# Modulation products with 32 equal moving columns and two more dummy matmuls ahead of the first attention unit

## Chip, cores, metric

One core of a Trainium2 chip. The metric is the device time of one execution in microseconds (us). Each execution also has a *span*, from the first to the last instruction that the profile records, and a granted TensorE clock (1.000 is full).

## The reference

One block of a conditioned transformer: a modulation vector of six slices from `c`, a layer norm scaled and shifted by it, attention with cached keys and values, and an MLP.

```python
mod = (_silu(c) @ w_mod).reshape(c.shape[0], 6, 1, -1)      # c: (1, 512), w_mod: (512, 3072)
sa, ca, ga, sb, cb, gb = (mod[:, 0].copy(), ..., mod[:, 5].copy())
h = _layernorm(x, axis=-1) * (1 + ca) + sa                  # x: (1, 2048, 512)
x = x + ga * _A_ref(h, A_k_cache, A_v_cache, A_wq, A_wo)    # 32 heads, 512 keys
h = _layernorm(x, axis=-1) * (1 + cb) + sb
x = x + gb * _B_ref(h, B_w1, B_w2)                          # 512 -> 1792 -> 512, ReLU
```

## The kernel before

TensorE works without a break once the first scores are computed. Everything that matters here is the way to that point: the two modulation slices `sa` and `ca` (32 products of one column each), the transposes of the first four normalised tiles, scaling and shifting (`mod_half`, on VectorE and ScalarE, whose results are the pieces hT that the Q projections read), the first Q projections in halves, the first scores. `warm(n)` issues dummy products of 512 columns that only keep TensorE busy.

```python
def warm(n, gate=(), bk=7):
    for i in range(n):
        mm(bank[bk], ones[:, :], ones[:, 0:1].to_broadcast([P, QB]), True, True, [R_ones] + list(gate), [bk], i == n - 1)

def mod_cols_mm(which, bk):                     # 4 x 2 x 4 = 32 products, all into one bank
    ...
                fs.append(lambda sl=sl, c2=c2, cc=cc, col=sl * DC + c2, last=last: mm(
                    bank[bk][:, col:col + 1], wm[sl][:, cc, c2 * P:(c2 + 1) * P], sc_bf[:, cc:cc + 1],
                    cc == 0 and sl == 0 and c2 == 0, last, [R_sc, wm_res(sl, cc)], [bk], last))

def mod_cols_evac(which, bk):                   # modc <- the eight columns + (0 or 1)
    ...
# --- the order of the start (cut to what the argument touches) ---
warm(10)                                        # first warm-up
silu_exp(5)
ln_stat(0); warm(3, [R_mv[0]]); ln_stat(1); warm(2, [R_mv[1]])
...
for f in mod_cols_mm(0, QBK): f()
ln_tposes(0, TB[0])
mod_cols_evac(0, QBK)
ln_tposes(1, TB[0])
warm(2, bk=1)                                   # the two dummies among the transposes
ln_norm(2)
mod_half(0, 0, DVE); mod_half(0, 2, ACT)
ln_tposes(2, TB[1]); ln_tposes(3, TB[1])
mod_half(0, 1, DVE); mod_half(0, 3, ACT)
q_half(0, 0, CC_ORDER, QBK)                     # four products, one for each hT piece
mod_half(1, 0, DVE); mod_half(1, 2, ACT); mod_half(1, 1, DVE); mod_half(1, 3, DVE)
q_evac_half(0, 0, QBK, ACT)                     # qT <- psQ on ScalarE
q_half(1, 0, CC_ORDER, 5); q_evac_half(1, 0, 5, ACT)
s_half(0, 0); s_half(1, 0)                      # the first score products
...
```

Of the kernel before, what the change touches and what calls it, by code (L numbers as in the profile page):

```python
# [9 lines left out]
ALU = mybir.AluOpType  # L10
# [127 lines left out]
def build_general(nc, es, A_x, A_k_cache, A_v_cache, A_wq, A_wo, B_x, B_w1, B_w2, c, w_mod, out, cfg=None):  # L138
# [27 lines left out]

    NQT = cfg.get("NQT", 4)
    NPB = cfg.get("NPB", 4)
# [11 lines left out]
    if True:  # L180
# [4 lines left out]
        def AL(name, n):  # L185
            lay[name] = (off[0], n)
            off[0] += n + (n % 2)
# [8 lines left out]
        AL("U", max(DC * 6 * D + G * KC * Dh, NOT * QB))  # L196
        AL("qT", NQT * QB)
        AL("Pb", NPB * pslot)
# [36 lines left out]
        def ring(name, n, sz):  # L235
            o = lay[name][0]
            return [arena[:, o + i * sz: o + (i + 1) * sz] for i in range(n)]
# [22 lines left out]
        oT = [arena[:, Ub + i * QB: Ub + (i + 1) * QB] for i in range(NOT)]  # L260
        qT = ring("qT", NQT, QB)
        Pb = ring("Pb", NPB, pslot)
# [66 lines left out]
        R_w2 = RL("w2", FC)  # L329
        R_qT = RL("qT", NQT)  # L330
        R_Pb = RL("Pb", NPB)
# [497 lines left out]
        def rec_qp(i, k):  # L829
# [11 lines left out]
            if k == DC - 1:  # L841
                qs = i % NQT
                if LN1_FOLD:
# [6 lines left out]
        def rec_qk(i, tl):  # L850
            b, h = units[i]
            g = h // R
            qs = i % NQT
            pbs = i % NPB
# [344 lines left out]
def build_fast(nc, es, top, A_x, A_k_cache, A_v_cache, A_wq, A_wo, B_x, B_w1, B_w2, c, w_mod, out, flag):  # L1199
    P = 128  # L1200
# [11 lines left out]
    DC = D // P  # L1212
# [10 lines left out]
    NPT = 3  # L1223
    NOS = 4
    NQT = 3
    VW = P + 8

    def T(name, shape, dt=BF):
        return es.enter_context(nc.sbuf_tensor(name, shape, dt))
# [6 lines left out]
    kT_sb = T("kT", [P, G, W])  # L1236
    v_sb = T("v", [P, G, KC, VW])
    hT = [T(f"hT{i}", [P, DC, QB]) for i in range(2)]
# [8 lines left out]
    wm = [wm01[:, :, 0:D], wm01[:, :, D:2 * D]] + [wmw[:, i * DC * D:(i + 1) * DC * D].rearrange("p (c n) -> p c n", c=DC) for i in range(2, 6)]  # L1247
# [12 lines left out]
    m01 = T("m01", [P, 2 * DC], F32)  # L1260
    sc_bf = T("sc_bf", [P, DC])
    sc_f = T("sc_f", [P, DC], F32)
    tmp = T("tmp", [P, DC], F32)
    modc = T("modc", [P, 4 * DC], F32)
# [17 lines left out]
    bank = [s_ps[0][:, 0, :], s_ps[0][:, 1, :], s_ps[1][:, 0, :], s_ps[1][:, 1, :], q_ps[:, :],  # L1282
            o_ps[:, 0:2, :].rearrange("p a b -> p (a b)"), o_ps[:, 2:4, :].rearrange("p a b -> p (a b)"), w_ps[:, :]]
# [3 lines left out]
    kb = KB(nc)  # L1287
    PE = kb.stream("pe", sem("s_pe"))
    ACT = kb.stream("act", sem("s_act"))
    DVE = kb.stream("dve", sem("s_dve"))  # L1290
# [22 lines left out]
    R_b = RL("bank", 8)  # L1313
# [9 lines left out]
    R_cf, R_m01 = Res("cf"), Res("m01")  # L1323
# [32 lines left out]
    def wm_res(sl, cc):  # L1356
        return R_wmc[cc] if sl < 2 else R_wm[sl]
# [15 lines left out]
    def mm(out_ap, lhsT, rhs, start, stop, reads, bk, signal):  # L1373
        kb.op(PE, lambda e: e.matmul(out_ap, lhsT, rhs, start=start, stop=stop), reads=reads, group_writes=[R_b[k] for k in bk], signal=signal)  # L1374

    def tpose(out_ap, in_ap, reads, bk, signal):
        kb.op(PE, lambda e: e.transpose(out_ap, in_ap, ident[:, :]), reads=list(reads) + [R_ident], group_writes=[R_b[k] for k in bk], signal=signal)  # L1377
# [4 lines that stand above are left out]
# [11 lines left out]
    def ln_norm(t):  # L1393
        b, tl = t // TPB, t % TPB
        kb.op(DVE, lambda e: e.tensor_scalar(xn[:, tl, :], x_sb[:, t, :], mv[:, t, 0:1], rstd[:, t:t + 1], op0=ALU.subtract, op1=ALU.mult),
              reads=[R_x[t], R_mv[t], R_rstd[t]], writes=[R_xn[tl]])
# [10 lines left out]
    def ln_tposes(tl, bks):  # L1407
        for cc in range(DC):
            bk = bks[cc]
            o = TO[tl // 2][cc] + tl % 2 * P  # L1410
            tpose(bank[bk].bitcast(BF)[:, o:o + P], xn[:, tl, cc * P:(cc + 1) * P], [R_xn[tl]], [bk], cc == DC - 1)
# [15 lines left out]
    def mod_cols_mm(which, bk):  # L1427
        fs = []
        for cc in range(DC):
            for sl in (0, 1):  # L1430
                for c2 in range(DC):
                    last = sl == 1 and c2 == DC - 1 and cc == DC - 1
                    fs.append(lambda sl=sl, c2=c2, cc=cc, col=sl * DC + c2, last=last: mm(
                        bank[bk][:, col:col + 1], wm[sl][:, cc, c2 * P:(c2 + 1) * P], sc_bf[:, cc:cc + 1],
                        cc == 0 and sl == 0 and c2 == 0, last, [R_sc, wm_res(sl, cc)], [bk], last))
        return fs

    def mod_cols_evac(which, bk):
        mo, r = which * 2 * DC, (R_moda, R_modb)[which]
        kb.op(DVE, lambda e: e.tensor_tensor(modc[:, mo:mo + 2 * DC], bank[bk][:, :2 * DC], m01[:, :], op=ALU.add), reads=[R_b[bk], R_m01], writes=[r])  # L1440

    def mod_part(sl, cc):
        dst, r = pr[sl - 2], R_pr[sl - 2]
# [135 lines left out]
    kb.op(POOL, lambda e: e.memset(cst[:, 3:4], -1.0), writes=[R_eps])  # L1579
    kb.op(POOL, lambda e: e.memset(v_sb[:, :, :, P:VW], 1.0), writes=[R_v1])  # L1580
    kb.op(POOL, lambda e: e.memset(m01[:, 0:DC], 0.0), writes=[R_m01])
# [13 lines left out]
    def rstd_pow(lo, hi):  # L1595
# [12 lines left out]
          reads=[R_x[t3], R_nmr, R_rstd[t3]], writes=[R_xn[t3]])  # L1608
# [8 lines left out]
    def q_evac_half(u, hf, bk, eng):  # L1617
# [4 lines left out]
        else:  # L1622
            kb.op(ACT, lambda e: e.activation(dst, src, ACTF.Copy), reads=[R_b[bk]], writes=w)

    fs = mod_cols_mm(0, QBK)
    for f in fs:
        f()
    ln_tposes(0, TB[0])
    mod_cols_evac(0, QBK)
    HB = QB // 2  # L1630
    R_half = [R_h0, R_hT[0]]

    def mod_half(hf, cc, eng):
        bk = TB[hf][cc]
        o = TO[hf][cc]
        src, dst = bank[bk].bitcast(BF)[:, o:o + HB], hT[0][:, cc, hf * HB:(hf + 1) * HB]
        sc, sh = modc[:, DC + cc:DC + cc + 1], modc[:, cc:cc + 1]
        if eng is DVE:
            kb.op(DVE, lambda e: e.tensor_scalar(dst, src, sc, sh, op0=ALU.mult, op1=ALU.add), reads=[R_b[bk], R_moda], writes=[R_half[hf][cc]])
        else:  # L1640
            kb.op(ACT, lambda e: e.activation(dst, src, ACTF.Identity, bias=sh, scale=sc), reads=[R_b[bk], R_moda], writes=[R_half[hf][cc]])  # L1641
# [12 lines left out]
              reads=[R_b[pr * 2], R_b[pr * 2 + 1]], writes=[R_PT[0][pr]])  # L1654

    ln_tposes(1, TB[0])
    warm(2, bk=1)
    ln_norm(2)
    mod_half(0, 0, DVE)
    mod_half(0, 2, ACT)  # L1660
    ln_tposes(2, TB[1])
    ln_tposes(3, TB[1])
    mod_half(0, 1, DVE)
    mod_half(0, 3, ACT)
    q_half(0, 0, CC_ORDER, QBK)
# [21 lines left out]
    for g in range(G):  # L1687
        for i, op in enumerate((ALU.max, ALU.min)):
            add((3, 5, 12, 16, 20, 24, 28, 32)[g], lambda g=g, i=i, op=op: kb.op(DVE, lambda e: e.tensor_reduce(vmax[:, i, g:g + 1], v_sb[:, g, :, 0:Dh], axis=AX.XY, op=op),
                                                             reads=[R_v[g]], writes=[R_vmax]))  # L1690
# [139 lines left out]
def bass_adaLN_cond__sliding_block_cached__dense_activation_relu__prompt_kernel(  # L1830
# [14 lines left out]
    with ExitStack() as top:  # L1845
        flag = top.enter_context(nc.sbuf_tensor("flag", [1, 8], mybir.dt.int32))
        with ExitStack() as es:
            kb, fast, cut, dma_cnt, flag_ev = build_fast(nc, es, top, *args, flag)
            sems = dict(kb.sems)
            meet = top.enter_context(nc.semaphore("s_meet"))  # L1850
# [84 lines left out]
```

## Time and profile before

| kernel before | |
|---|---|
| time, median of the first 3 runs | 560.38 us (560.31 to 560.55) |
| span of the traced execution | 559.0 us |
| TensorE busy | 99% of the span |
| first score product starts at | 11.65 us |

How to read it: with TensorE busy to the end, a change of the start is worth what it moves the first score product by. The lines that show it are in the prediction.

### The profile page before, as it was taken

What the parts mean: (1) busy time and instruction counts of PE and PEld (TensorE: products, weight loads), DVE (VectorE), ACT (ScalarE), POOL (GpSimd) and SP (SyncE); (2) the same over time, 40 slices, a digit from 0 to 9 for tenths busy, and PEclk for the clock granted to TensorE, in tenths of its full rate; (3) what the DMA queues carried; (4) which work ended last, traced back from release to release, by engine and by line L of the source; (5) the groups of instructions that cost most, each with busy time, mean ns of one, the idle gap of its engine ahead of it and who ended that gap; (6) DMA issues with size and microseconds to landing.
All of it is one profiled execution on the core that took longest, in us unless ns stands there. A gap on an engine that the chain in (4) does not pass through costs nothing.

```text
span 559.0 us, 9759 instructions
## 1 busy us (share of the span) xinstructions
PE 553.9 (99%) x4139; PEld 316.6 (57%) x4139; DVE 254.9 (46%) x556; ACT 349.4 (63%) x455; POOL 52.7 (9%) x50
## 2 busy tenths in 40 slices
PE   8999999999999999999999999999999999999997
PEld 4665555555555555555555555555555554444444
DVE  5555555553546544335445443333354438322134
ACT  5986666666666666666666666666666644432500
POOL 2000022004400000033000000332000000000000
PEclk9999999999999999999999999999999999999999
DMA  9999763422224244353353312121123110200001
GB/s 234 296 196 185 136 166 42 114 43 73 38 41 74 39 84 106 61 130 58 96 95 57 76 40 39 39 38 38 39 39 76 39 29 0 50 28 21 21 29 48
DMA packets 113356, 42.66 MB, mean 76 GB/s; under 512 B 93976, under 2 KB 112152, under 8 KB 113304
## 3 DMA queue, kind: packets, MB, share of 16 engines
q1 hardware_dynamic: 112584, 41.08, 35.5%
q10 hardware_dynamic: 720, 0.89, 0.5%
q8 instruction: 33, 0.54, 0.4%
q14 instruction: 19, 0.16, 0.1%
HBM read 18.35 MB, written 2.10 MB: 37 GB/s over the span
## 4 chain that ended last, share of the span: by engine, by line
PE 98%; DMA 1%; SPq 0%; DVE 0%; issue 0%
PE psS L1374 29%; PE psO L1374 27%; PE psQ L1374 23%; PE psW L1374 20%; DMA wmw<-in_w_mod_dram 1%; SPq L1303 0%; PE psS L1377 0%; PE psO L1377 0%; DVE PT L1752 0%; DVE PT L1754 0%; PE psW L1377 0%
## 5 line engine op out<-in xcount | busy, mean ns | idle before, releaser
L1498 ACT ACTIVATE PT<-psS 128x1024 bf16<-128x1024 f32 x254 | 260.4, 1027 | 127.0 <-PE psS L1374 126.9
L1374 PE MATMUL psS<-qT,kT 128*128 128x512 bf16 (+1 forms) x516 | 151.8, 377 | 0.1
L1374 PEld LDWEIGHTS psO<-v,PT 128*128 128x128 bf16 x2048 | 126.6, 98 | 30.2
L1374 PE MATMUL psO<-v,PT 128*128 128x129 bf16 x2048 | 137.0, 220 | 0.0
L1374 PE MATMUL psW<-wo,oT 128*128 128x512 bf16 x512 | 130.6, 379 | 0.0
L1374 PE MATMUL psQ<-hT,wq 128*128 128x512 bf16 (+1 forms) x508 | 129.6, 377 | 0.0
L1508 DVE RECIPROCAL rinv<-psO 128x4 f32<-128x4 f32 x128 | 23.3, 182 | 225.3 <-PE psO L1374 225.3
L1509 DVE TENSOR_TENSOR o<-psO,rinv 128x512 bf16<-128x512 f32 x128 | 88.5, 691 | 4.7 <-DVE rinv L1508 0.3
L1374 PEld LDWEIGHTS psS<-qT,kT 128*128 128x128 bf16 x516 | 50.0, 98 | 58.7 <-issue 0.4
L1374 PEld LDWEIGHTS psQ<-hT,wq 128*128 128x128 bf16 x508 | 49.7, 98 | 59.0 <-ACT hT L1641 0.2
L1490 ACT ACTIVATE qT<-psQ 128x512 bf16<-128x512 f32 x125 | 73.9, 591 | 0.0
L1741 ACT ACTIVATE wq<-psS 128x512 bf16<-128x512 f32 x56 | 33.4, 597 | 49.1 <-PE psS L1374 49.1
L1374 PEld LDWEIGHTS psW<-wo,oT 128*128 128x128 bf16 x512 | 45.0, 98 | 32.9 <-DVE acc L1531 1.2
L1531 DVE TENSOR_TENSOR acc<-psW,acc 128x512 f32<-128x512 f32 x48 | 33.2, 691 | 6.7 <-PE psW L1374 6.7
L1374 PE MATMUL psO<-wmw,wq 128*128 128x512 bf16 (+1 forms) x168 | 32.9, 352 | 0.0
L1534 POOL TENSOR_TENSOR acc<-acc,gaf 128x512 f32<-128x512 f32 x12 | 15.6, 1301 | 146.9 <-DVE acc L1531 139.8
L1390 POOL TENSOR_TENSOR rstd<-rstd,cst 128x4 f32<-128x4 f32 x7 | 7.2, 1027 | 216.6 <-DVE rstd L1389 216.6
L1752 DVE TENSOR_TENSOR PT<-psO,gbf 128x512 f32<-128x512 f32 (+1 forms) x12 | 7.5, 624 | 40.4 <-PE psO L1374 40.4
L1374 PE MATMUL psS<-h2T,wmw 128*128 128x512 bf16 x112 | 25.3, 379 | 0.0
L1374 PEld LDWEIGHTS psO<-wmw,wq 128*128 128x128 bf16 x168 | 15.4, 98 | 16.5
L1374 PE MATMUL psS<-hT,wmw 128*128 128x512 bf16 x112 | 24.5, 379 | 0.0
L1384 DVE BATCH_NORM_STATS2 st<-x 128x6 f32<-128x512 bf16 x31 | 21.1, 680 | 3.7 <-DMA x<-in_A_x_dram 3.7
(93 smaller groups left out, 197.1 us busy)
## 6 DMA issues: line engine op xcount, KB each, us to landing
wo<-in_A_wo_dram SPq DMA_DIRECT2D x4, 1024.0 KB, 5.9
wq<-in_A_wq_dram SPq DMA_DIRECT2D x7, 512.0 KB, 4.5
wmw<-in_B_w_dram SPq DMA_DIRECT2D x14, 256.0 KB, 3.1
wmw<-in_w_mod_dram SPq DMA_DIRECT2D x4, 512.0 KB, 5.0
oT<-o SPq DMA_TRANSPOSE x128, 2.4
out_dram<-PT SPq DMA_DIRECT2D x15, 128.0 KB, 1.7
x<-in_A_x_dram SPq DMA_DIRECT2D x3, 512.0 KB, 4.3
v<-in_A_v_cache_dram SPq DMA_DIRECT2D x8, 128.0 KB, 4.5
```

What stands on the lines that cost most here:

```text
L1374: kb.op(PE, lambda e: e.matmul(out_ap, lhsT, rhs, start=start, stop=stop), reads=reads, group_writes=[R_b[k] for k in bk], signal=signal)
L1384: kb.op(DVE, lambda e: e.bn_stats(st[:, t, :], x_sb[:, t, :]), reads=[R_x[t]], writes=[R_st[t]])
L1390: kb.op(POOL, lambda e: e.tensor_tensor(rstd[:, sl], rstd[:, sl], cst[:, 0:1].to_broadcast([P, hi - lo]), op=ALU.pow), reads=R_rstd[sl] + ...
L1490: kb.op(ACT, lambda e: e.activation(qT[u % NQT][:, :], bank[bk], ACTF.Copy), reads=[R_b[bk]], writes=[R_qT[u % NQT]])
L1498: kb.op(ACT, lambda e: e.activation(PT[u % NPT][:, pr * 2:pr * 2 + 2, :], s_ps[pr][:, :, :], ACTF.Exp, scale=scale), reads=[R_b[pr * 2], R ...
L1508: kb.op(DVE, lambda e: e.reciprocal(rinv[:, u, :], o_ps[:, :, P]), reads=[R_b[5], R_b[6]], writes=[R_rinv])
L1509: kb.op(DVE, lambda e: e.tensor_tensor(o_sb[u % NOS][:, :, :], o_ps[:, :, 0:P], rinv[:, u, :].unsqueeze(2).to_broadcast([P, TPB, P]), op=A ...
L1531: kb.op(DVE, lambda e: e.tensor_tensor(acc[:, tl, :], bank[WBK], acc[:, tl, :], op=ALU.add), reads=[R_b[WBK], R_acc[tl]], writes=[R_acc[tl]])
L1534: kb.op(eng, lambda e: e.tensor_tensor(acc[:, tl, :], acc[:, tl, :], gaf[:, :], op=ALU.mult), reads=[R_acc[tl], R_ga], writes=[R_acc[tl]])
L1741: kb.op(ACT, lambda e: e.activation(h1T[b % 2][:, fc, :], bank[bk], ACTF.Relu), reads=[R_b[bk]], writes=[R_h1[b % 2][fc]], pre=all_events( ...
L1752: kb.op(DVE, lambda e: e.tensor_tensor(yt[i][:, c0:c1], bank[bk][:, c0:c1], gbf[:, c0:c1], op=ALU.mult), reads=[R_b[bk], R_gb], writes=[R_ ...
```

## The change

The intent, as the code suggests, is to give TensorE more work in the thin stretch before the first unit, for the sake of its clock; what a thinner start does to the clock is measured in experiment 11 (0.994 to 0.997 in five of six executions). Each modulation product streams the same column 32 times, and the eviction picks the first of each 32; a third dummy stands before the transposes of tile 2, and one more after those of tile 3.

```diff
+    NR = 32
     ...
-                        bank[bk][:, col:col + 1], wm[sl][...], sc_bf[:, cc:cc + 1],
+                        bank[bk][:, col * NR:(col + 1) * NR], wm[sl][...], sc_bf[:, cc:cc + 1].to_broadcast([P, NR]),
     ...
-        ... bank[bk][:, :2 * DC], m01[:, :], op=ALU.add) ...
+        ... bank[bk][:, :2 * DC * NR].rearrange("p (c r) -> p c r", r=NR)[:, :, 0], m01[:, :], op=ALU.add) ...
     ...
     ln_tposes(1, TB[0])
-    warm(2, bk=1)
+    warm(3, bk=1)
     ...
     ln_tposes(3, TB[1])
+    warm(1, bk=1)
```

More of the change, by code (lines that the diff above doesn't have):

```diff
@@ L1433, in mod_cols_mm @@
                     fs.append(lambda sl=sl, c2=c2, cc=cc, col=sl * DC + c2, last=last: mm(
-                        bank[bk][:, col:col + 1], wm[sl][:, cc, c2 * P:(c2 + 1) * P], sc_bf[:, cc:cc + 1],
+                        bank[bk][:, col * NR:(col + 1) * NR], wm[sl][:, cc, c2 * P:(c2 + 1) * P], sc_bf[:, cc:cc + 1].to_broadcast([P, NR]),
                         cc == 0 and sl == 0 and c2 == 0, last, [R_sc, wm_res(sl, cc)], [bk], last))
@@ L1439, in mod_cols_evac @@
         mo, r = which * 2 * DC, (R_moda, R_modb)[which]
-        kb.op(DVE, lambda e: e.tensor_tensor(modc[:, mo:mo + 2 * DC], bank[bk][:, :2 * DC], m01[:, :], op=ALU.add), reads=[R_b[bk], R_m01], writes=[r])
+        kb.op(DVE, lambda e: e.tensor_tensor(modc[:, mo:mo + 2 * DC], bank[bk][:, :2 * DC * NR].rearrange("p (c r) -> p c r", r=NR)[:, :, 0], m01[:, :], op=ALU.add), reads=[R_b[bk], R_m01], writes=[r])
     def mod_part(sl, cc):
```

## The prediction

> **What bounds the kernel now.** I read the page first, then the chain of waits, then the sums of waits per engine, then the timeline of the first 24 us.
>
> The page gives the span and its bound:
>
> ```profile
> span 559.0 us, 9759 instructions
> PE 553.9 (99%) x4139; PEld 316.6 (57%) x4139; DVE 254.9 (46%) x556; ACT 349.4 (63%) x455; POOL 52.7 (9%) x50
> PEclk9999999999999999999999999999999999999999
> PE 98%; DMA 1%; SPq 0%; DVE 0%; issue 0%
> ```
>
> TensorE is busy for 99% of the span and carries 98% of the chain that ended last. In the sums of waits it has only two entries, 1.1 us at the very start and 0.6 us for the modulation weights; after about 12 us it waits for nothing that shows. So a shift of the moment at which TensorE enters its dense stretch moves the end by the same amount, and nothing later can absorb it. The change touches only what lies before that moment. The chain of waits in its early part shows where that moment is (start, length, what):
>
> ```profile
> 2.05 6.77 DMA wmw<-in_w_mod_dram
> ...
> 8.87 0.35 PE psQ L1374 x8
> 9.22 0.47 PE psS L1377 x8
> 9.69 0.43 PE psS L1374 x2
> ...
> 10.57 0.52 PE psQ L1374 x4
> 11.09 0.44 PE psO L1374 x4
> 11.52 0.13 issue
> 11.65 0.60 PE psS L1374 x4
> 12.25 0.44 PE psQ L1374 x4
> ```
>
> A transfer of modulation weights lands at 8.82; then come the last eight modulation products (psQ), the transposes of tiles 0 and 1, two dummies (psS from L1374), the transposes of tiles 2 and 3 (cut here), the first half of two Q projections, and at 11.65 the first score products. From there on every piece joins the next without a gap. The question is therefore by how much 11.65 moves.
>
> The timeline shows who waits there (start, length, engine, line, operation, tiles, count, wait):
>
> ```profile
> 8.86 0.27 PEld L1374 LDWEIGHTS psQ<-sc_bf,wmw 128*128 128x128 bf16 x8 [0.29 <-DMA wmw<-in_w_mod_dram]
> 8.87 0.35 PE L1374 MATMUL psQ<-sc_bf,wmw 128*128 128x1 bf16 x8 [0.21 <-DMA wmw<-in_w_mod_dram]
> 9.34 0.40 DVE L1395 TENSOR_SCALAR xn<-x,mv,rstd 128x512 bf16<-128x512 bf16 x1
> 9.53 0.60 PE L1374 MATMUL psS<-ones 128*128 128x512 bf16 x2
> 9.73 1.02 ACT L1641 ACTIVATE hT<-psS,modc 128x256 bf16<-128x256 bf16 x2 [0.61 <-PE psS L1377]
> 9.80 0.26 PEld L1377 LDWEIGHTS psO<-ident,xn 128*128 128x128 bf16 x2 [0.17 <-DVE xn L1395]
> 9.96 0.27 PE L1377 MATMUL psO<-ident,xn 128*128 128x128 bf16 x2
> 10.40 0.68 PE L1374 MATMUL psQ<-hT,wq 128*128 128x256 bf16 x4
> 10.80 0.10 PEld L1374 LDWEIGHTS psQ<-hT,wq 128*128 128x128 bf16 x1 [0.18 <-ACT hT L1641]
> 11.12 0.38 ACT L1623 ACTIVATE qT<-psQ 128x256 bf16<-128x256 f32 x1
> ```
>
> Two things matter. The transposes of tile 2 have their data at 9.74 and their weight load starts at 9.80, but the first of them only runs at 9.96: the two dummies, streaming from 9.53 to 9.96, already hold them up. And the fourth Q product waits for ScalarE's second hT piece, which ends at 9.73 + 1.02 = 10.75; until then TensorE has a small hole. The score products at 11.65 follow ScalarE's copy of qT, which ends at 11.50; the chain calls the gap "issue".
>
> [...]the dummies at the start are issued 0.43 us apart (weight loads at 5.73, 6.14, 6.56) and last 590 ns on the mean, while the two at 9.53 last 380 ns. The row of granted clock shows none of this, so spacing and duration are the evidence. From 6.9 us on everything is fast: Q products of 512 columns last 379 ns over the whole run. [...]eight end 0.35 us after the first starts, one lasts 164 ns, so (350 - 164)/7 = 27 ns apart. [...]the transposes here last 218 ns[...].
>
> **The change part by part.**
>
> *32 columns instead of one, 32 products.* [...]The first 24 products are followed by waits for transfers (0.21 to 0.40 us), so nothing of theirs shows.[...]
>
> *The strided eviction of modc.* Still eight values per partition, on VectorE, at 9.26 for 0.17 us. hT work at 9.73 waits for the transposes, which end at 9.30 + 0.39 = 9.69; modc is ready at 9.43. Some 0.3 us of slack: 0 us.
>
> *Third dummy before the transposes of tile 2.* [...](600 - 380) = 0.22 us by the two at 9.53. No hole to fall into: the first transpose moves from 9.96 to 10.18, the last (spaced 0.055) from 10.35 to 10.57, and its result from 10.57 to 10.79.
>
> *One dummy after the transposes.* It starts at about 10.62 and takes 0.22, so the first Q product moves from 10.40 to 10.84 (+0.44). Now ScalarE's 10.75 is past before its product comes: the four run 0.108 us apart, the fourth at 10.84 + 3 x 0.108 = 11.16 in place of 10.80. The hole of about 0.08 us has been used up, and +0.36 us remains.
>
> *What follows.* The Q result moves from 11.08 to 11.44, ScalarE's copy from 11.12 to 11.48 (its preceding hT piece, from 10.64, moves only by 0.22), the score products from 11.65 to 12.01. VectorE's three hT pieces for the second half move from 10.61 to 10.83 and end at 11.88, well before the Q products that need them, at 12.08 + 0.36 = 12.44. The 0.30 us in which TensorE stands between 11.35 and 11.65 is the latency of ScalarE's copy behind the delayed product, and moves along with it; it absorbs nothing.
>
> Sum: 0.44 for two dummies, less 0.08 absorbed[...]: **+0.37 us**, 560.38 + 0.37 = **560.75 us**, +0.07%.
>
> **The rivals.**
>
> *The clock.* The change looks meant to keep the array's activity up in the thin stretch from 7 to 10 us[...]. [...]Against it: the traced execution stays fast through that stretch and beyond, it took 560.87 us itself, no less than the others, and the three timed runs lie within 0.24 us; an occasional fallback would scatter them by over 1 us. One in ten that some gain of this kind appears.
>
> *All hidden.* The dummies fall in time in which TensorE waits anyway: 560.4. For it: TensorE does stand 0.08 + 0.30 us between 9.53 and 11.65, nearly as much as is added. Against it: the larger hole lies behind a dependency on the delayed product, as told. One in seven that the shift is under 0.15 us.
>
> [...]
>
> *A slower eviction.* Doubling its 0.17 us stays inside its slack of 0.3 us: no effect.
>
> **Range and chances.** [...]the scatter within one set of runs is 0.24 us and another set may sit some tenths of a us elsewhere. Eight in ten: 559.8 to 561.5. A change of 2% would be 11.2 us[...]: 0.99 for within 2%, the rest split evenly.
>
> **What would show it right or wrong.** In the changed trace, relative to the landing of the last modulation weights: products of 32 columns still 25 to 27 ns apart, about 178 ns each; three dummies, then the transposes of tile 2 0.22 us later; the fourth Q product without a wait for ScalarE; the first score products 0.36 us later; and the same products as before from there on. I am wrong if the products are spaced 40 ns, if the score products start as early as before, or if matmuls that last 379 ns here have another duration. The landing of the modulation weights itself can move the start by tenths of a us from execution to execution; that belongs to no part of the change.

The sum came to +0.37 us, 560.75 us: 0.44 - 0.08 = +0.36 us, as it stands there, and +0.01 us for the columns. Estimated from the trace: the two dummies of 512 columns run (600 - 380) = 220 ns apart, so 32 columns take about 220 x 32/512 = 14 ns. That is less than the 25 to 27 ns at which the products of one column start behind each other (the trace before has seven starts 25 ns apart from 8.91 to 9.06 us), so an estimate of 0.01 us for the last product alone. The clock rival supposed that executions without a profiler fall back to half rate in the thin stretch; the low end of my range was an estimate of mine. Three figures were measured: the transposes' 218 ns are the duration of the products of 128 columns at the end of the kernel (219 ns), products of 32 columns last 178 ns (experiment 3), and the six executions of the kernel before at a granted clock of 0.997 have spans 1.0 us or more above the full-clock ones of the same rounds.

## The result, and the profile after

| | before | after |
|---|---|---|
| median | 560.35 us (560.02 to 560.66, 6 runs) | 560.97 us (560.93 to 561.68, 6 runs) |
| ratio | | 1.0015, 95% interval 1.0002 to 1.0028 |
| spans | 559.0 us in the traced execution | 558.4 to 558.8 us, traced: 558.7 us |

A ratio is the mean time of one kernel's fast runs over that of the other's of the same rounds, so not quite the ratio of the medians quoted. The time lies in the predicted range; the difference of the medians is +0.62 us where +0.37 us was predicted.

The page of the changed kernel:

```profile
span 558.7 us, 9689 instructions
PE 549.4 (98%) x4067; PEld 316.4 (57%) x4141; DVE 255.1 (46%) x556; ACT 349.7 (63%) x455; POOL 52.8 (9%) x50
PE 97%; issue 1%; DVE 1%; DMA 1%
```

TensorE seems to be busy 4.5 us less. That is no gain: there are 4141 weight loads and only 4067 matmul records; some records are missing, and the matmuls that remain last as long as before (379 ns with 512 columns and 220 ns with 129 in both traces). But one thing here is odd: the changed kernel has the *shorter* traced span and the longer time.

The chain of waits of the changed kernel, early part (start, length, what):

```profile
0.79 3.87 DMA x<-in_A_x_dram
...
8.08 0.33 DVE xn L1396
...
8.46 0.72 PE psS L1378 x8
9.18 0.05 issue
9.23 0.60 PE psS L1375 x2
...
10.27 0.22 PE psS L1375
10.49 0.44 PE psQ L1375 x4
10.93 0.44 PE psO L1375 x4
11.36 0.13 issue
11.49 0.60 PE psS L1375 x4
```

The chain does not begin with the modulation weights now, but with the load of x and the layer norm on VectorE: in this execution the modulation weights landed earlier. That is scatter between executions (one of the unchanged kernel, traced later in experiment 1, looks the same: its 32 modulation products run from 7.29 us in 1.08 us, without a wait for the weights), and it moves the start by tenths of a us (first score product at 11.65 and at 11.30 us in the two traces of the kernel before). So absolute times of two traces must not be compared. I measure from the first hT piece on ScalarE instead, which waits for both.

The timeline of the changed kernel (start, length, engine, line, operation, count):

```profile
9.21 1.02 ACT L1642 ACTIVATE hT<-psS,modc 128x256 bf16<-128x256 bf16 x2 [0.18 <-PE psS L1378]
9.23 0.60 PE L1375 MATMUL psS<-ones 128*128 128x512 bf16 x2
9.67 0.27 PE L1378 MATMUL psO<-ident,xn 128*128 128x128 bf16 x2
10.11 0.38 PE L1375 MATMUL psS<-ones 128*128 128x512 bf16 x1
10.33 0.60 PE L1375 MATMUL psQ<-hT,wq 128*128 128x256 bf16 x4
10.96 0.38 ACT L1624 ACTIVATE qT<-psQ 128x256 bf16<-128x256 f32 x1
```

Three dummies stand before the transposes of tile 2: their weight loads are there three times, from 8.96, and one of their matmul records is among the missing ones.

| from the first hT piece on ScalarE to | before | predicted | after |
|---|---|---|---|
| first transpose of tile 2 | 9.96 - 9.73 = 0.23 | 0.45 | 9.67 - 9.21 = 0.46 |
| first Q product | 10.40 - 9.73 = 0.67 | 1.11 | 10.33 - 9.21 = 1.12 |
| first score product | 11.65 - 9.73 = 1.92 | 2.28 | 11.49 - 9.21 = 2.28 |

The four Q products take 0.60 us now, not 0.68, and no wait for ScalarE stands before the fourth: the hole is used up. From the first score product to the last group of products it is 554.07 - 11.65 = 542.42 us before and 553.91 - 11.49 = 542.42 us after. So the inside of the span does what was predicted, +0.36 us. The time grew by more, and the question is where the rest lies.

It lies outside the span. Time less span, which I call the *rest* below, is 560.87 - 559.0 = 1.9 us in the one execution of the kernel before whose span I had then, and 2.2 to 3.2 us in the six of the changed kernel.

### The profile page after: what moved, and what is told of

Same layout as the page of the kernel before. It is cut to its first block, busy times and chain, and to the rows that moved or that the text cites. A ratio compares the mean times of both kernels' runs of the same rounds, so it can differ in the third digit from the quotient of the medians.

```text
span 558.7 us, 9689 instructions
## 1 busy us (share of the span) xinstructions
PE 549.4 (98%) x4067; PEld 316.4 (57%) x4141; DVE 255.1 (46%) x556; ACT 349.7 (63%) x455; POOL 52.8 (9%) x50
## 4 chain that ended last, share of the span: by engine, by line
PE 97%; issue 1%; DVE 1%; DMA 1%
PE psS L1375 29%; PE psO L1375 27%; PE psQ L1375 22%; PE psW L1375 19%; DMA x<-in_A_x_dram 1%; DVE st L1385 0%; PE psS L1378 0%; DVE mv L1386 0%; PE psO L1378 0%; DVE xn L1396 0%; DVE rstd L1594 0%; DVE PT L1754 0%; DVE PT L1756 0%; DVE tmp L1425 0%; DVE sc_bf L1426 0%
## 5 line engine op out<-in xcount | busy, mean ns | idle before, releaser
L1375 PE MATMUL psW<-wo,oT 128*128 128x512 bf16 x452 | 118.1, 379 | 3.2
```

The costliest lines, as they stand in the source:

```text
L1375: kb.op(PE, lambda e: e.matmul(out_ap, lhsT, rhs, start=start, stop=stop), reads=reads, group_writes=[R_b[k] for k in bk], signal=signal)
```

## Experiments

Twelve kernels, all timed in five rounds, each giving six executions, beside eleven of the kernel before. The runs before of the three calls have spans of 558.1 to 558.9 us at full clock (means 558.30, 558.42 and 558.54 us) and a rest of 1.70 to 1.91 us in every one of the 33. The theory: the change costs +0.36 us inside the span by its dummies, and something outside it. The rivals: the columns carry a part; or all beyond 0.36 us is noise; and, for the outside, number of instructions against place and kind. I count these in pairs: a TensorE product and its weight load.

**1. The kernel before, unchanged.**

> The kernel before, unchanged, as a measure of the noise and of its spans. Every theory: ratio 1.000 within 0.001. Mine (two dummies cost 0.36 us, the rest of the measured +0.62 us is scatter of the start, set by when the x and modulation transfers land): the spans of its executions scatter by some tenths of a us, the traced distance from ScalarE's first hT piece to the first score product is 1.92 us as before, and the time less the span is the same 2.3 to 3.0 us as the changed kernel has it. Rival (something outside the span has grown with the changed program, since the traced changed kernel has a span 0.3 us SHORTER than the traced kernel before): time less span stays near the 1.9 us of the one traced execution.

Measured: 560.35 us against 560.22, ratio 0.9996 (0.9982 to 1.0011), mean span 558.53 us, rest 1.79 to 1.91 us, hT piece to score product 9.38 to 11.30 = 1.92 us. My expectation of the rest (2.3 to 3.0 us if mine, 1.9 if the rival) fell for the rival. The mean span of six executions of the same program differs by 0.2 us from that of the runs beside it; smaller differences of such means say nothing.

The same rounds brought a surprise: three of the eleven executions beside it had a granted clock of 0.997, spans of 559.7 to 560.0 us and times of 561.5 to 561.8 us. The record calls them fast runs too, and its ratios include them; where I compare means below, I take the full-clock executions (0.999 or 1.000) alone. More of that under 9 to 12.

**2. The changed kernel, unchanged.**

> The changed kernel again, unchanged. Mine: +0.3 to +0.5 us over the kernel before in time and in mean span (ratio 1.0006 to 1.0009), hT piece to first score product 2.28 us. Rival (the first measurement of +0.62 to +0.84 us is the true size): +0.6 us or more again, ratio 1.0011 to 1.0015.

Measured: 561.28 us against 560.22, ratio 1.0013 (0.9998 to 1.0027). Mean span 558.68 us, rest 2.32 to 3.31 us, mean 2.67; hT piece to score product 9.02 to 11.30 = 2.28 us. Against the eight full-clock executions beside it (mean time 560.12, mean span 558.30, rest 1.82) the mean time of 561.35 us is +1.23 us: **+0.38 us of span and +0.85 us of rest**. The ratio is smaller than that because the three executions at 0.997 are in its denominator. My +0.3 to +0.5 us holds for the span and fell for the time, which is nearer to the rival's size.

**3. Columns alone.** The change without its two dummies:

```diff
-    warm(3, bk=1)
+    warm(2, bk=1)
...
     ln_tposes(3, TB[1])
-    warm(1, bk=1)
```

> 32 equal columns, the dummies as before. Mine: the products stay 25 to 27 ns apart[...], so ratio 1.0000 (0 to +0.05 us), hT piece to score product 1.92 us. Rival (the missing 0.2 to 0.4 us comes from the columns, by weight load and stream that do not overlap or by the strided eviction): products 40 ns apart, +0.1 to +0.4 us, ratio 1.0002 to 1.0007.

Measured: 560.00 us, ratio 0.9989 (0.9975 to 1.0003), mean span 558.28 us (-0.02), rest 1.79 to 1.86 us, hT piece to score product 9.66 to 11.59 = 1.93 us. The products by form, in the kernel before and then with columns alone (count, busy us, mean ns):

```profile
L1374 PE MATMUL psQ<-sc_bf,wmw 128*128 128x1 bf16 x32 | 1.2, 164 | 0.6 <-DMA wmw<-in_w_mod_dram 0.6
```

```profile
L1375 PE MATMUL psQ<-sc_bf,wmw 128*128 128x32 bf16 x32 | 1.4, 178 | 0.6 <-DMA wmw<-in_w_mod_dram 0.5
```

A product lasts 14 ns longer. The timeline with columns alone has the last eight, which wait for their weights, and the transposes behind them:

```profile
8.80 0.37 PE L1375 MATMUL psQ<-sc_bf,wmw 128*128 128x32 bf16 x8 [0.15 <-DMA wmw<-in_w_mod_dram]
9.02 0.61 PE L1378 MATMUL psS<-ident,xn 128*128 128x128 bf16 x8
```

(370 - 178)/7 = 27 ns apart, as with one column, and the transposes start 0.22 us behind the first of them (before: 9.08 - 8.87 = 0.21). So the columns cost nothing that shows in this trace or in the ratio. The rival that they carry a part falls.

**4. Dummies alone.** The kernel before with `warm(3, bk=1)` and the later `warm(1, bk=1)`.

> The two more dummies, the products with one column. Mine: the whole effect of the change, +0.36 us, ratio 1.0006, hT piece to first score product 2.28 us. Rival (columns carry a part): clearly less than the changed kernel of the same rounds.

Measured: 561.40 us, ratio 1.0015 (1.0000 to 1.0030): the whole of the change's effect. Mean span 558.87 us, hT piece to score product 9.51 to 11.78 = 2.27 us, rest 2.34 to 3.23 us. The distance is the one that I expected; the ratio of 1.0006 fell, since the longer rest, too, comes with the dummies.

**5. Two dummies of one column.** The same number of instructions without their time:

```diff
     warm(2, bk=1)
+    mm(bank[1][:, 0:1], ones[:, :], ones[:, 0:1], True, True, [R_ones], [1], True)
...
     ln_tposes(3, TB[1])
+    mm(bank[1][:, 0:1], ones[:, :], ones[:, 0:1], True, True, [R_ones], [1], True)
```

> The kernel before with two more dummies in the places of the change's, but of ONE column each: the same number of TensorE instructions as the changed kernel, almost none of the time. In both theories the distance from the first hT piece to the first score product stays 1.92 to 1.94 us (two times 25 ns fall into the hole of 0.08 us). Theory A (what grows outside the span hangs on the number of TensorE instructions, as the instruction fetches after the last product suggest): time less span 2.3 or 3.2 us as with the two long dummies, so +0.5 to +1.0 us over the kernel before. Rival (it hangs on the time that the dummies take, or on the phase of the end): time less span 1.8 to 1.9 us, and the time of the kernel before within 0.1 us.

Measured: 561.14 us, ratio 1.0015 (1.0002 to 1.0028), mean span 558.32 us (-0.10), hT piece to score product 8.93 to 10.86 = 1.93 us, **rest 2.38 to 3.24 us**. The span is that of the kernel before, and the time is not. The rest hangs on the instructions that were added, not on the time that TensorE spends on them.

**6. Only the later dummy.** The kernel before with `warm(1, bk=1)` after the transposes of tile 3.

> Only the dummy after the transposes of tile 3, products with one column. Inside the span: 0.22 us less the hole of 0.08 us, so hT piece to score product 2.06 us. Theory A (instruction count): one pair of instructions instead of two; time less span is at 1.8 us if the step lies beyond it, or at 2.3 us or more if one pair is enough; a value between would speak against a step. Rival: 1.8 us.

Measured: hT piece to score product 9.07 to 11.13 = 2.06 us, as expected; rest 1.70 to 1.87 us; mean time 560.37 us, +0.16 us over the ten full-clock executions beside it (560.21). So a dummy at this place costs 0.14 us after the hole, and this one pair of instructions leaves the rest alone; the two pairs of the change do not.

**7. The change with two dummies fewer at the very start.** `warm(10)` becomes `warm(8)`; the number of instructions is that of the kernel before.

> The changed kernel with eight in place of ten dummies in the first warm-up, which ends in idle time: the columns and the two later dummies stay, the number of TensorE instructions is that of the kernel before. Theory A (a step outside the span that hangs on the number of TensorE instructions): time less span falls from 2.2 to 3.3 us to 1.8 us; mean span stays 0.3 to 0.4 us over that of the kernel before's full-clock executions; time 560.5 to 560.7 us. Rival (the growth outside the span belongs to the place or the kind of the added instructions): time less span stays at 2.2 us or more.

Measured: 560.47 us against 560.33, ratio 1.0002 (0.9987 to 1.0018). **Rest 1.82 to 1.94 us**: gone, with columns and later dummies in place. hT piece to score product 9.09 to 11.37 = 2.28 us, as in the change. Two of the six executions had a span of 559.5 and 559.6 us at a granted clock of 1.000; that figure doesn't show the slow start (in the trace of the kernel before it reads 1.00 from 0 to 5 us, where the dummies come 0.43 us apart and not 0.22), so a longer slow start is possible; but I have no trace of such an execution, and leave it open. The other four have a mean span of 558.58 us, +0.04 us over the nine full-clock executions beside them (558.54), and all six 558.90 us, +0.36 us. I had expected +0.3 to +0.4 us. With a scatter of such means of 0.2 us (experiment 1) the spans don't settle it; the distance of 2.28 us does.

**8. Seven more pairs, in idle time.** One of the ten first dummies is replaced by eight of one column.

```diff
-    warm(10)
+    warm(9)
+    for i in range(8):
+        mm(bank[7][:, 0:1], ones[:, :], ones[:, 0:1], True, True, [R_ones], [7], i == 7)
```

> The kernel before with one of the ten first dummies replaced by eight of one column: seven more pairs of TensorE instructions, in time that is idle anyway; nothing else. Span as before. Theory A as a step: time less span 2.2 to 3.3 us, as with two more. As a cost per instruction: 0.2 to 0.7 us for each pair, so 3 us or more over 1.8. Rival (place or kind): 1.8 us.

Measured: 560.28 us, ratio 0.9994 (0.9980 to 1.0008), span 558.42 us, rest 1.75 to 1.91 us. My theory in its simple form, more instructions than some number, falls. What is left, in pairs of TensorE instructions against the kernel before: -5 (experiments 11 and 12), -2 (9 and 10), 0, +1 and +7 have a rest of 1.7 to 1.9 us in every execution, and +2 (the change, dummies alone, two tiny ones) 2.2 us or more in every execution. So it is neither the time of the added products nor their mere number. Place alone is not it either: in experiment 7 the change's own dummies stay where they are, and the long rest is gone. Two pairs in the idle time at the start, with nothing else changed, were not run.

The tails of the traces differ in their instruction fetches. Here are those from 559.5 us on, in the traced execution of the kernel before, then of the changed kernel, then with two tiny dummies, then with seven more pairs (queue: packets, MB, share):

```profile
q14 instruction: 1, 0.01, 0.5%
```

```profile
q14 instruction: 2, 0.02, 1.6%
```

```profile
q14 instruction: 2, 0.02, 1.7%
```

```profile
q14 instruction: 1, 0.01, 0.9%
```

The changed kernel and the one with two tiny dummies fetch once more on this queue; the second trace of the changed kernel, with a rest of 3.3 us, has five such fetches. But the trace of dummies alone, with a rest of 2.6 us, has one only, so the count of fetches isn't the whole of it. The fetches shown above have 8 KB each (five of them 0.04 MB). The other queue of instructions, q8, has 33 packets with 0.54 MB on the page of the kernel before, 16 KB each. On q8 six traces have one fetch each between 558 and 560 us, with a long rest (the changed kernel twice, dummies alone) or a short one (the kernel before twice, columns alone); the window of 559.5 us cuts some of them off.

I had a reading of the +2 pairs by the way in which the program's end is fetched; no trace or run shows it. Nor is a fetch shown to cost the time; in the trace of the kernel before, the one on q14 comes 1.9 us after the span's end, which is as long as the whole rest of that execution. Why +2 pairs lengthen the rest stays open.

**9. Without the two dummies among the transposes.** `warm(2, bk=1)` is deleted.

Theory A here, a guess of mine: the three executions at 0.997 come of too little TensorE work around the transposes.

> Neither of the two dummies between the transposes, products with one column: less TensorE activity around the transposes. Where the clock stays full, hT piece to score product is 1.92 us, since the fourth Q product waits for ScalarE anyway. Theory A (the three of eleven executions of the kernel before with a granted clock of 0.997 and a span longer by 1.6 us[...]): here a third of the executions or more have a clock of 0.997 and a span of 559.7 to 560.1 us. Rival (those three were an accident of the chip that has nothing to do with the dummies): none to one in six. Time less span 1.8 us or less.

Measured: 560.25 us against 560.22, ratio 0.9998 (0.9986 to 1.0010), hT piece to score product 9.08 to 11.00 = 1.92 us; none of six at 0.997, where I had expected a third. The expectation fell. The dummies before cost nothing and show no use in six executions.

**10. The same with columns.**

> The same without dummies, products with 32 columns[...]. Theory A ([...]the columns count as activity): fewer executions at 0.997 than without dummies and with one column, none to one in six, and the rest at the time of the columns alone, 560.0 us. Rival (columns of so short products do not count): as many at 0.997 as without dummies and with one column.

Measured: 560.33 us, ratio 0.9999 (0.9987 to 1.0011), none of six at 0.997, 9.35 to 11.27 = 1.92 us. With none in experiment 9 either, this tells nothing about the columns.

**11. A truly thin stretch.** The five dummies behind the first layer-norm statistics are deleted from the kernel before:

```diff
     ln_stat(0)
-    warm(3, [R_mv[0]])
     ln_stat(1)
-    warm(2, [R_mv[1]])
```

The question is whether a thin start is what the executions at 0.997 suffer from. Of the expectation's two cases, the first holds if it is.

> The kernel before without the five dummies that follow the first two layer-norm statistics (between 5.5 and 7.4 us), products with one column: it has a truly thin stretch from about 5 us to 8.5 us. [...]most executions here have a granted clock of 0.997 or less and a span of 559.7 us or more, and the profile shows products at half rate. If those executions are something else, the spans stay at 558.1 to 558.8 us and the clock at 0.999 to 1.000.

Measured: 561.97 us against 560.33, ratio 1.0023 (1.0008 to 1.0038). Five of six executions at 0.994 to 0.997, with spans of 559.5 to 560.6 us; the sixth has a span of 560.5 us at 1.000. The trace has one of them. Its timeline:

```profile
9.68 0.63 PE L1374 MATMUL psS<-ones 128*128 128x512 bf16 x1 [0.22 <-issue]
10.86 0.31 PE L1377 MATMUL psO<-ident,xn 128*128 128x128 bf16 x1
10.96 1.06 PE L1374 MATMUL psQ<-hT,wq 128*128 128x256 bf16 x4
12.59 0.60 PE L1374 MATMUL psS<-qT,kT 128*128 128x256 bf16 x4
```

and its table by windows (length, busy times, granted clock, DMA share, GB/s):

```profile
8.00:10.00 2.00, 1.56 (x25) 1.16 (x23) 1.81 (x8) 1.31 (x3) 0.86 (x3) 0.76 1.04 207
10.00:12.00 2.00, 2.00 (x14) 1.61 (x13) 1.02 (x4) 1.08 (x3) 0.00 (x0) 0.50 1.14 306
12.00:14.00 2.00, 2.00 (x18) 1.60 (x16) 0.60 (x2) 1.62 (x4) 0.00 (x0) 0.89 1.18 312
```

A dummy lasts 0.63 us where it lasted 0.38, a transpose 0.31 where it lasted 0.22, and four Q products 1.06. A mean of 0.76 over the first 2 us is (1 - 0.76) x 2 / 0.5 = 0.96 us at half rate, then 2 us, then (1 - 0.89) x 2 / 0.5 = 0.44 us: together 3.4 us at half rate, from about 9.0 to 12.4 us. So here a thinner start comes with a stretch at half rate. An execution at 0.997 has lost as much by the same sum, 0.003 x 560 / 0.5 = 3.4 us; where in the kernel before it loses it, no trace shows, since no traced execution of it was one.

**12. The thin stretch with columns.**

> The same with products of 32 columns. If the columns count as activity, as the change seems to intend, clearly fewer executions at 0.997 or less than with one column (under a half of its share). If they do not count or do not suffice, the same share.

Measured: 561.84 us, ratio 1.0018 (1.0002 to 1.0033). Four of six executions at 0.996 or 0.997 against five of six; the traced one is at half rate from about 8.7 to 12.1 us although its products have 32 columns. By the span it is five of six (the one at 0.999 has 560.6 us; only one, with 558.9 us, is as short as the kernel before) against six of six. The columns do not suffice to keep the clock here; such counts in six say no more.

**The clock in the kernel before.** Of its 40 executions with a known clock (33 beside the experiments, six in experiment 1, and the first traced one) six stand at 0.997, with spans 1.0 us or more above every full-clock one of the same rounds (559.7 to 560.4 against at most 558.9 us). The changed kernel has none in twelve. At six in 40 the chance of none in twelve is (34/40)^12 = 0.14 if executions are independent, and the two kernels with less TensorE work at the start than the kernel before (experiments 8 and 9) have none in twelve either. That the change cures those executions is neither shown nor excluded.

## Why the prediction was right, and what it missed

- *TensorE bounds the end, so the first score product's delay is the change's cost inside the span.* Right: 542.42 us from that product to the last group in both traces.
- *Columns: still 25 to 27 ns apart, about 178 ns each.* Right (experiment 3): 27 ns, 178 ns, transposes at 0.22 in place of 0.21 us; without effect on the time (0.9989, interval across 1).
- *Third dummy: 0.22 us with no hole to fall into. Later dummy: 0.22 us less a hole of 0.08 us before the fourth Q product.* Right: the three distances in the table are met within 0.01 us, and the later dummy alone gives 2.06 - 1.92 = 0.14 us.
- *The larger hole behind ScalarE's copy absorbs nothing.* Right: it moves along. What the chain calls "issue" there is 0.13 us in both kernels.
- *The slower eviction stays in its slack.* Right: it lasts 0.16 us in the trace of the changed kernel (0.17 before).
- *The clock rival.* I held it against that the traced execution stays fast and three timed runs agree. It was less remote than that: a stretch at half rate exists (experiment 11, with the five early dummies gone: 3.4 us, granted clock 0.50 from 10 to 12 us), and something of the same size strikes one execution of the kernel before in six or seven, at 1.6 us or so; three runs were too few to see it. It moves the mean of the kernel before, hardly the median.
- *Two rates.* The trace has them: dummies 0.43 us apart at the start, 0.22 us at 9.53. Where the change from one to the other lies differs: in the trace before, the dummies run from 1.10 us with hardly a gap, and the weight loads at 6.14 and 6.56 us are still 0.42 us apart, over 5 us at half rate; in the changed kernel's trace the last three of the first ten, at 3.95, 4.17 and 4.38 us, are 0.22 us apart. (The loads that are named in the prediction are 0.41 and 0.42 us apart; 0.43 us is the distance of those before them.) Nothing in the sum hangs on it.
- *The step that was missing.* The sum went from 560.38 us by +0.37 us as if time less span were fixed. It is 1.8 us in the kernel before and 2.2 to 3.3 us in the changed kernel, for a reason that is open, but is not the dummies' work: two tiny dummies have it, and the change with two dummies fewer at the start doesn't. This term is as large as the effect that I did work out, or larger: +0.85 us on the mean in experiment 2. The range held because it was wide, not because I had seen this.

No version beat both kernels clearly; the columns alone have the lowest median (560.00 us), with an interval that includes no difference.

## What to carry to other kernels

When a change is worth tenths of a us, compare time less span before explaining the time, and run a kernel that adds the same number of instructions without their work: two tiny pairs alone were worth 1.1 us of time outside the span on the mean here, up to 1.4 us. Between traces, measure distances from an event that both share, not absolute times, since the landing of the first loads moves the start (by 0.35 us between two traces of one kernel here). In this kernel a dummy matmul cost its 0.22 us wherever TensorE's own work stood behind it, less what a later wait covered: 0.14 us for the later one (experiment 6), nothing for the two of the kernel before (experiment 9).
